# Reordering the head of a fused softcap attention and maxout MoE kernel: loads, casts and fill units ahead of the first crossbar transposes

## The chip, the cores and the metric

The kernel runs on one core of one Trainium2 chip. Times are device microseconds (us) of that core, each the median of several executions of one compiled kernel; the profile is of one execution. All executions in this study were of the fast state; within it those of one kernel still spread (the kernel before from 356.5 to 360.8 us on one chip), so a profiled execution need not be a typical one. Engines: TensorE (PE, with its weight loads PEld), VectorE (DVE), ScalarE (ACT), GpSimd (POOL), SyncE (SP, which issues nearly all DMAs; SPq marks its queue).

## The reference

```
scores = q @ k^T / sqrt(64)                 # 8 batches, 12 heads, 448 positions, 64 wide, fp32
scores = cap * tanh(scores / cap)           # cap = 30
attn   = softmax(scores)                    # exp, divided by the sum
x      = (attn @ v), heads joined           # 3584 x 768
out    = maximum(x @ w1, x @ w2) @ w_out    # 768 -> 1024 -> 768
```

The kernel computes maximum(a, b) as b + relu(a − b): it needs wd = w1 − w2 ("subtract") for the relu branch, and wm = w2 @ w_out ("premultiply"), worked out on the chip once.

## The kernel before

Two heads make a pair, three pairs a group g (16 groups), two pairs a quad t (24 quads). For groups 0 and 1 q and k are transposed by TensorE, for groups from 2 on by a DMA through the crossbar (`cross(g)`). What can be run between quads is kept as a queue of single TensorE instructions: first the transposes of w2 and the premultiply, then the MoE matmuls of each batch. `F(n)` takes n units off it. All orders are given by hand; each engine runs its instructions in the order of the program.

```python
    def load(g, what, n0=0, n1=L):       # q, k or v of pairs n0..n1 of group g, by SyncE's queue
        ...
    def cast(eng, g, what, n0=0, n1=L, halves=(0, 1)):   # fp32 -> bf16 into the buffers that matmuls read
        ...
    def load_w1(c):                      # 512 KB, by SyncE's queue
        w1_in[c] = ...
        nc.sync.dma_start(out=w1_in[c], in_=x_rows(moe_w1, c))

    def subtract(c, eng=nc.vector):
        eng.tensor_sub(wd_sb[:, c, :], w1_in[c], w2b[:, c, :])

    def cross(g):                        # q and k of a group through the crossbar
        nc.sync.dma_start_transpose(
            out=qkT_of(g).rearrange("p n j c -> p (n j) c"), in_=kqf[g % 2].rearrange("p n j c -> p (n j c)")
        )

    def add(t, ab, step):                # sums of exponentials on VectorE, for quads from NS = 3 on
        if t < NS or t >= NQ:
            return
        ...                              # six tensor_add a quad; total(t) then needs 4 matmuls in place of 16

    # ---- the order at the head ----
    load(1, "k"); load(1, "q"); load(0, "v")                # (cut: group 0's q and k, w2, w_out)
    ...
    load(1, "v")
    load(2, "k")
    load(2, "q")
    for c in range(KC):                                     # KC = 6
        load_w1(c)
    ...
    cast(nc.gpsimd, 1, "v")
    cast(nc.gpsimd, 2, "k")
    cast(nc.gpsimd, 2, "q")
    ...                                                     # (cut: quad 1's scores)
    cross(2)
    load(3, "k")
    load(3, "q")
    load(2, "v")
    ...
    for t in range(1, NQ):
        more = t + 1 < NQ
        F(24 if t == 2 else 0)
        if t > 1 and more:
            scores(t + 1, 0)                                # t == 2: quad 3, the first that needs cross(2)
        if t > 1:
            ex(t, 3)
            F(6)
        ...
        if t == 2:
            cast(nc.gpsimd, 3, "k")
            cast(nc.gpsimd, 3, "q")
            cross(3)                                        # needed by scores(4, 1), at t == 3
            for c in range(4, KC):
                subtract(c, nc.gpsimd)
        ...
        F(8 if t > 1 else 0)
        add(t, 1, 0)
        F(2 if t > 1 else 0)
        if more:
            scores(t + 1, 1)
            ex(t + 1, 0)
        ...                                                 # (cut: more adds, scores and fill)
        total(t)
        if more:
            scores(t + 1, 3)
            ex(t + 1, 2)
        else:
            F(12)
        normalize(t, values(t))                             # t == 1 is the first that needs v of group 1
        if t % 3 == 2:
            fill_q.append(moe(t // 3))
        F(3)
    F(10 ** 9)                                              # the rest of the queue
```

Of the kernel before, what the change touches and what calls it, by code (L numbers as in the profile page):

```python
# [10 lines left out]
def kernel(  # L11
# [11 lines left out]
    nc = tc.nc  # L23
# [10 lines left out]
    KC, FC = DM // P, DF // P  # L34
    NP = H // 2
    N = B * NP
    L = 3
# [64 lines left out]
    def rows(t, b, h0, h1):  # L102

        return t[b, h0:h1, :, :].rearrange("h (r j) d -> (h r) (j d)", j=R7)
# [4 lines left out]
    def raw_of(g, what):  # L109
        if (g, what) not in raw:  # L110
            if (g, what) == (1, "v"):
                raw["unused"] = raw_tile(what)
            raw[g, what] = raw_tile(what)
        t = raw[g, what]
        m = t[:, : 2 * L * NJ * D].rearrange("p (h c) -> p h c", c=NJ * D)
        l = t[:, 2 * L * NJ * D :].rearrange("p (h d) -> p h d", d=D)
        return t, m, l

    def load(g, what, n0=0, n1=L):
        b, p = divmod(g * L, NP)  # L120
        h0, h1 = 2 * (p + n0), 2 * (p + n1)
        src = {"k": k, "q": q, "v": v}[what]
        t, m, l = raw_of(g, what)
        if g < NT:
            nc.sync.dma_start(
                out=t[:, n0 * S : n1 * S].rearrange("p (n c) -> p n c", c=S),
                in_=rows(src, b, h0, h1).rearrange("(n p) c -> p n c", p=P),
            )
            return
        nc.sync.dma_start(  # L130
            out=m[:, 2 * n0 : 2 * n1, :],
            in_=src[b, h0:h1, 0 : NJ * P, :].rearrange("h (p j) d -> p h (j d)", j=NJ),
        )
        if what == "q":
            nc.sync.dma_start(
                out=l[half(b), 2 * n0 : 2 * n1, :],
                in_=src[b, h0:h1, NJ * P : S, :].rearrange("h p d -> p h d"),
            )
        else:
            for par in range(2):  # L140
                nc.sync.dma_start(
                    out=l[64 * par : 64 * par + 64, n0:n1, :],
                    in_=src[b, h0 + par : h1 : 2, NJ * P : S, :].rearrange("h p d -> p h d"),
                )

    def cast(eng, g, what, n0=0, n1=L, halves=(0, 1)):

        b = g * L // NP
        x, m, l = raw_of(g, what)
        if what == "v" and g < NT:  # L150

            x = x[:, : L * S].rearrange("p (n c) -> p n c", c=S)
            for h in halves:
                r = slice(64 * h, 64 * h + 64)
                for a in range(2):
                    eng.tensor_copy(
                        vp[g % 2][64 * a : 64 * a + 64, h::2, :, :].rearrange("p n j d -> p n (j d)"),
                        x[r, :, NJ * D * a : NJ * D * (a + 1)],
                    )
                eng.tensor_copy(vl[g % 2][r, :, r], x[r, :, 2 * NJ * D :])  # L160
            return
        if what == "v":
            eng.tensor_copy(
                vp[g % 2][:, 2 * n0 : 2 * n1, :, :].rearrange("p h j d -> p h (j d)"), m[:, 2 * n0 : 2 * n1, :]
            )
            for par in range(2):
                r = slice(64 * par, 64 * par + 64)
                eng.tensor_copy(vl[g % 2][r, n0:n1, r], l[r, n0:n1, :])
            return
        if g < NT:  # L170

            x = x[:, n0 * S : n1 * S].rearrange("p (n c) -> p n c", c=S)
            if what == "q":
                eng.tensor_copy(flat(g)[:, n0:n1, Q0 : Q0 + S], x)
                return
            eng.tensor_copy(flat(g)[:, n0:n1, : NJ * P], x[:, :, : NJ * P])
            for par in range(2):
                r = slice(64 * par, 64 * par + 64)
                eng.tensor_copy(kf[g % 2][r, n0:n1, 3, r], x[r, :, NJ * P :])
            return  # L180
        o = b % 2 if what == "q" else 0
        t = (kf if what == "k" else qf)[g % 2]
        eng.tensor_copy(  # L183
            t[:, n0:n1, o : o + NJ, :].rearrange("p n j (h d) -> p n h j d", h=2),
            m[:, 2 * n0 : 2 * n1, :].rearrange("p (n h) (j d) -> p n h j d", h=2, d=D),
        )
        if what == "q":
            eng.tensor_copy(
                t[half(b), n0:n1, 3 * (1 - o), :],
                l[half(b), 2 * n0 : 2 * n1, :].rearrange("p (n h) d -> p n (h d)", h=2),  # L190
            )
        else:
            for par in range(2):
                r = slice(64 * par, 64 * par + 64)
                eng.tensor_copy(t[r, n0:n1, 3, r], l[r, n0:n1, :])
# [24 lines left out]
    def load_w1(c):  # L220
        w1_in[c] = opool.tile([P, DF], f32, name="osb") if c < OB else w1x[:, (c - OB) * DF : (c - OB + 1) * DF]
        nc.sync.dma_start(out=w1_in[c], in_=x_rows(moe_w1, c))
# [227 lines left out]
    def F(n):  # L450
        rate[1] += n * rate[0]
        while rate[1] >= 1 and fill_q:
            try:
                next(fill_q[0])
                rate[1] -= 1
            except StopIteration:
                fill_q.pop(0)
        if not fill_q:
            rate[1] = 0.0
# [53 lines left out]
    for c in range(2, KC):  # L513
        load_w2(c)
    cast(nc.gpsimd, 0, "v", halves=(1,))
    load(1, "v")
    load(2, "k")
    load(2, "q")
    for c in range(KC):
        load_w1(c)  # L520

    first = {}
# [1 line left out]
    def premultiply_first(f0, f1):  # L524
        if f0 == 0:
            first[0] = pv_psum.tile([P, 512], f32, name="pv")
            first[1] = pv_psum.tile([P, 512], f32, name="ss")
        for f in range(f0, f1):
            for half in range(2):
                nc.tensor.matmul(  # L530
                    first[half][:, : DM // 2],
                    w2T[0][:, f * P : (f + 1) * P],
                    wo_sb[:, f, half * (DM // 2) : (half + 1) * (DM // 2)],
                    start=(f == 0), stop=(f == FC - 1),
                )
        if f1 == FC:
            for half in range(2):
                nc.vector.tensor_copy(
                    wm_sb[:, 0, half * (DM // 2) : (half + 1) * (DM // 2)], first[half][:, : DM // 2]
                )  # L540
# [7 lines left out]
    scores(1, 0)  # L548
    transposes(3)
    cast(nc.vector, 0, "v", halves=(0,))  # L550
    cast(nc.gpsimd, 1, "v")
    cast(nc.gpsimd, 2, "k")
    cast(nc.gpsimd, 2, "q")
    premultiply_first(0, 2)
    scores(1, 1)
    ex(1, 0)
# [8 lines left out]
    cross(2)  # L565
    load(3, "k")
    load(3, "q")
    load(2, "v")
    premultiply_first(6, 8)
    for c in range(1, KC):  # L570
# [10 lines left out]
    for t in range(1, NQ):  # L581
        i = 2 * t
        more = t + 1 < NQ
        F(24 if t == 2 else 0)
        if t > 1 and more:
            scores(t + 1, 0)
        if t > 1:
            ex(t, 3)
            F(6)
        if t in crosses:  # L590
            cross(crosses[t])
        if t == 2:
            cast(nc.gpsimd, 3, "k")
            cast(nc.gpsimd, 3, "q")
            cross(3)
            for c in range(4, KC):
                subtract(c, nc.gpsimd)
        if t == 3:
            cast(nc.gpsimd, 3, "v")
        if t > 2:  # L600
            extra(i)
# [6 lines that stand above are left out]
        F(4)  # L608
        add(t, 1, 1)
        F(4)  # L610
        if t == 2:
            cast(nc.gpsimd, 2, "v")
            load(3, "v")
        add(t, 0, 2)
        F(4)
        add(t, 1, 2)
        F(4)
        if more:
            scores(t + 1, 2)
            ex(t + 1, 1)  # L620
            F(5)
            add(t + 1, 0, 0)
        if t == 1:
            for c in range(4):
                subtract(c, nc.gpsimd)
        if t == 2:
            extra(4)
            extra(5)
        if t > 2:
            extra(i + 1)  # L630
        F(5)
# [4 lines that stand above are left out]
            add(t + 1, 0, 1)  # L636
        else:
            F(12)
        normalize(t, values(t))
        if casts[t]:  # L640
            nc.gpsimd.tensor_copy(mark, x_of(t, 1)[:1, :1])  # L641
            for g, what in casts[t]:
                cast(nc.gpsimd, g, what)
# [3 lines that stand above are left out]
# [34 lines left out]
```

## Time and profile before

| | before |
|---|---|
| time, median of 3 runs | 359.78 us (359.24 to 359.86) |
| span of the profiled execution | 357.5 us |
| TensorE busy, idle | 336.5, 21.0 us |
| ScalarE's last instruction ends | 306.3 us |
| from there to the end ("the tail") | 51.2 us |
| first crossbar transpose: issued, landed | 38.7, 47.9 us |
| second crossbar transpose: issued, landed | 56.1, 63.4 us |

A timeline row is: start, duration (both us, merged over the instructions at the end of the row, "x14"), engine, line, operation, result <- operands, shapes, and in brackets how long the engine sat idle before it and what released it. "us to landing" in the DMA view counts from the start of the issue to the last byte. The rows that matter are shown in the prediction; the second transpose is this row of the queue's timeline:

```profile
56.10 3.64 SPq L279 DMA_TRANSPOSE qkT<-kqf  x1
```

and the DMA view of that stretch gives it 7.3 us to landing, so 63.4.

### The profile page before, as it was taken

Reading aid. Unit: us, or ns where it says so; the run is one execution under the profiler, and the core shown is the slowest. Engines: PE = TensorE matmul, PEld = TensorE weight load, DVE = VectorE, ACT = ScalarE, POOL = GpSimd, SP = SyncE. Lnnn points to the kernel's source line nnn. Section 1 sums busy time; section 2 is a strip of 40 time slices with the busy share of each in tenths; the row PEclk is TensorE's granted clock in tenths of the full one; section 3 lists DMA queues with packets and bytes.
Section 4 is the critical chain, followed back from the end, with each engine's and each line's share of the span. In section 5 each row is a group of like instructions: output and inputs, shape, how many; then the busy total and the mean of one; then the engine's idle time right before and its main releaser. Section 6 shows DMA issues by size and latency. Waiting matters only on the chain.

```text
span 357.5 us, 6788 instructions
## 1 busy us (share of the span) xinstructions
PE 336.5 (94%) x2710; PEld 163.5 (46%) x2710; DVE 227.3 (64%) x410; ACT 281.5 (79%) x265; POOL 108.3 (30%) x172
## 2 busy tenths in 40 slices
PE   3899869899999999999999999999999999999996
PEld 2444424444444444445444554444445444455563
DVE  4336607777767776786688565976786667843421
ACT  3989639899999999999999999999999999200000
POOL 6554848231244124303430443034304400000000
PEclk9999969999999999999999999999999999999999
DMA  7999997948796869675977498948982511012022
GB/s 252 245 251 246 345 253 168 271 92 209 109 300 156 196 126 303 193 167 96 294 217 166 81 266 261 197 94 233 272 190 57 155 72 65 0 46 89 0 90 88
DMA packets 103200, 61.79 MB, mean 173 GB/s; under 512 B 62336, under 2 KB 98176, under 8 KB 103168
## 3 DMA queue, kind: packets, MB, share of 16 engines
q1 hardware_dynamic: 101216, 58.21, 62.6%
q0 software_dynamic: 1952, 3.15, 4.9%
q8 instruction: 21, 0.34, 0.4%
q14 instruction: 11, 0.09, 0.1%
HBM read 42.47 MB, written 11.01 MB: 150 GB/s over the span
## 4 chain that ended last, share of the span: by engine, by line
PE 42%; ACT 36%; DMA 13%; DVE 7%; issue 1%; SPq 0%; DVEq 0%; ACTq 0%
ACT expo L314 17%; ACT tanh L307 16%; PE mm L406 13%; PE mm L421 10%; DMA kr<-in_k_dram 9%; PE mm L418 8%; PE s L306 4%; ACT tanh L309 3%; DMA qkT<-kqf 3%; DVE gT L410 2%; PE pv L372 2%; PE ss L372 2%; DMA osb<-in_moe_w_dram 1%; DVE esum L333 1%; PE mm L243 1%
## 5 line engine op out<-in xcount | busy, mean ns | idle before, releaser
L314 ACT ACTIVATE expo<-tanh 128x1792 bf16<-128x1792 bf16 (+1 forms) x96 | 144.8, 1509 | 0.1
L307 ACT ACTIVATE tanh<-s 128x896 bf16<-128x896 f32 x144 | 124.2, 914 | 17.9 <-PE s L306 16.0
L421 PE MATMUL mm<-wo_sb,gT 128*128 128x384 bf16 x448 | 86.8, 327 | 0.0
L406 PE MATMUL mm<-xT,wd_sb 128*128 128x448 bf16 x384 | 80.2, 353 | 4.1 <-DVE gT L410 3.0
L418 PE MATMUL mm<-wm_sb,xT 128*128 128x384 bf16 x336 | 66.7, 327 | 0.2 <-DVE gT L410 0.2
L421 PEld LDWEIGHTS <-gT 128*128 128x128 bf16 x448 | 42.0, 98 | 34.2 <-issue 8.0
L406 PEld LDWEIGHTS <-wd_sb 128*128 128x128 bf16 x384 | 35.9, 98 | 44.1 <-issue 13.8
L425 DVE COPY osb<-mm 128x384 f32<-128x384 f32 x56 | 31.0, 554 | 37.0 <-PE mm L421 36.6
L306 PE MATMUL s<-qkT 64*128 64x448 bf16 x288 | 43.6, 371 | 7.7 <-DMA qkT<-kqf 4.2
L335 DVE TENSOR_TENSOR esum<-expo 128x896 bf16<-128x896 bf16 x42 | 29.4, 699 | 32.7 <-ACT expo L314 32.2
L410 DVE TENSOR_SCALAR gT<-mm 128x448 bf16<-128x448 f32 x64 | 39.6, 621 | 14.2 <-PE mm L406 13.8
L641 POOL COPY mark<-xT 1x1 bf16<-1x1 bf16 x18 | 3.2, 179 | 147.5 <-DVE xT L394 122.0
L418 PEld LDWEIGHTS <-xT 128*128 128x128 bf16 x336 | 31.8, 98 | 26.7 <-issue 6.6
L309 ACT ACTIVATE tanh<-s 128x896 bf16<-128x896 f32 x24 | 22.0, 916 | 6.0 <-PE s L301 5.5
L333 DVE TENSOR_TENSOR esum<-esum,expo 64x896 bf16<-64x896 bf16 x42 | 25.9, 617 | 0.9
L337 DVE TENSOR_TENSOR esum<-esum,expo 128x896 bf16<-128x896 bf16 x42 | 25.6, 610 | 0.3
L306 PEld LDWEIGHTS <-qkT 64*128 64x128 bf16 x288 | 9.7, 95 | 31.6 <-issue 24.2
L358 DVE STREAM_TRANSPOSE st<-ss 128x448 f32<-128x448 f32 x24 | 15.6, 649 | 8.8 <-PE ss L356 6.4
L372 PEld LDWEIGHTS <-vp 128*32 128x32 bf16 x576 | 13.3, 96 | 16.2 <-issue 8.3
L183 POOL CAST kqf<-kr 128x1152 bf16<-128x1152 f32 x14 | 15.9, 1138 | 9.0 <-DMA kr<-in_k_dram 5.0
L372 PE MATMUL pv<-expo,vp 128*32 128x448 bf16 x288 | 18.1, 356 | 0.0
L372 PE MATMUL ss<-expo,vp 128*32 128x448 bf16 x288 | 17.8, 352 | 0.0
(70 smaller groups left out, 275.5 us busy)
## 6 DMA issues: line engine op xcount, KB each, us to landing
kr<-in_k_dram SPq DMA_DIRECT2D x14, 576.0 KB, 6.6
qr<-in_q_dram SPq DMA_DIRECT2D x14, 576.0 KB, 7.1
vr<-in_v_dram SPq DMA_DIRECT2D x14, 576.0 KB, 4.9
out_dram<-osb SPq DMA_DIRECT2D x20, 384.0 KB, 4.7
out_dram<-osb SPq DMA_DIRECT2D x16, 192.0 KB, 4.2
osb<-in_moe_w_dram SPq DMA_DIRECT2D x4, 512.0 KB, 8.5
gT<-in_moe_w_dram POOLq DMA_DIRECT2D x6, 256.0 KB, 12.3
wo_sb<-in_moe_w_out_dram POOLq DMA_DIRECT2D x4, 384.0 KB, 16.2
```

What stands on the lines that cost most here:

```text
L306: nc.tensor.matmul(s[:, h, :S], k0[r, j * P : (j + 1) * P], qTn[r, :])
L307: nc.scalar.activation(tanh[t, p][:, 2 * m : 2 * m + 2, :], s[:, :, :S], AF.Tanh, scale=scale / cap)
L309: nc.scalar.activation(tanh[t, p][:, 0:2, :], s[:, :, :S], AF.Tanh, scale=scale / cap)
L314: nc.scalar.activation(expo[t, p], tanh[t, p][:, 0:n, :], AF.Exp, scale=float(cap))
L333: nc.vector.tensor_add(d, d, expo[t, 2][r, :, :])
L335: nc.vector.tensor_add(d, e_of(t, ab, 1 if ab else 0), e_of(t, ab, 2 if ab else 1))
L372: nc.tensor.matmul(ps[r, :S], vp[g % 2][:, 2 * n + h, j, u::2], e_of(t, ab, j)[:, h, :], start=(j == 0), stop=False,)
L406: nc.tensor.matmul(ps[:, :S], wd_sb[:, c, f * P : (f + 1) * P], x[:, c, cs], start=(c == 0), stop=(c == KC - 1))
L410: nc.vector.tensor_relu(g[:, f, cs], ps[:, :S])
L418: nc.tensor.matmul(ps[:, : DM // 2], x[:, c, ts], wm_sb[:, c, hs], start=(c == 0), stop=False)
L421: nc.tensor.matmul(ps[:, : DM // 2], g[:, f, ts], wo_sb[:, f, hs], start=False, stop=(f == FC - 1))
L425: nc.vector.tensor_copy(osb[:, hs], ps[:, : DM // 2])
```

## The change

The intent: the transpose that TensorE waits for should have its operands earlier (k and q of group 2 loaded ahead of two thirds of v of group 1, and cast ahead of that v), should not stand behind all of w1 (three of six chunks go behind it), and the fill kept ahead of quad 3 is cut from 24 units to 8, since the wait would be shorter. The whole diff:

```diff
     cast(nc.gpsimd, 0, "v", halves=(1,))
-    load(1, "v")
+    load(1, "v", 0, 1)
     load(2, "k")
     load(2, "q")
-    for c in range(KC):
+    load(1, "v", 1, L)
+    for c in range(3):
         load_w1(c)
...
     cast(nc.vector, 0, "v", halves=(0,))
-    cast(nc.gpsimd, 1, "v")
     cast(nc.gpsimd, 2, "k")
     cast(nc.gpsimd, 2, "q")
+    cast(nc.gpsimd, 1, "v")
...
     load(3, "k")
     load(3, "q")
+    for c in range(3, KC):
+        load_w1(c)
     load(2, "v")
...
-        F(24 if t == 2 else 0)
+        F(8 if t == 2 else 0)
...
-            for c in range(4, KC):
+            for c in range(3, KC):
                 subtract(c, nc.gpsimd)
...
         if t == 1:
-            for c in range(4):
+            for c in range(3):
                 subtract(c, nc.gpsimd)
```

Below, "the v part", "the w1 half" and "the 8 units" name its three parts.

## The prediction

> **What bounds the kernel now.** The kernel first loads and casts three heads' pairs at a time (a group), turns q and k, then runs 24 attention quads t (scores, tanh, exp, values), and lets a static queue of "fill" matmuls (the MoE part) run between them, so many units at each place. I read first the shares on the page and the waits of TensorE (us in total, times, longest):
>
> ```profile
> PE 336.5 (94%) x2710; PEld 163.5 (46%) x2710; DVE 227.3 (64%) x410; ACT 281.5 (79%) x265; POOL 108.3 (30%) x172
> ```
> ```profile
> PE s L306 <- DMA qkT<-kqf: 4.2, 1, 4.2
> ...
> PE mm L406 <- DVE gT L410: 3.0, 4, 1.3
> ```
>
> TensorE is busy nearly everywhere, so time can only come from its idle stretches and from the clock. The largest idle stretch is one wait of 4.2 us, for the first crossbar transpose (group 2's q and k, needed by quad 3). TensorE's timeline around it (start us, us, what, idle before):
>
> ```profile
> 37.45 0.55 PE L306 MATMUL s<-qkT 64*128 64x448 bf16 x4
> 37.94 0.75 PE L372 MATMUL pv<-expo,vp 128*32 128x448 bf16 x12
> ...
> 43.20 0.48 PE L243 MATMUL mm<-wo_sb,w2T 128*128 128x384 bf16 x2 [0.20 <-DVE wm_sb L248]
> 47.90 0.93 PE L306 MATMUL s<-qkT 64*128 64x448 bf16 x4 [4.21 <-DMA qkT<-kqf]
> 48.76 4.52 PE L243 MATMUL mm<-wo_sb,w2T 128*128 128x384 bf16 x14
> ...
> 53.32 0.55 PE L306 MATMUL s<-qkT 64*128 64x448 bf16 x4
> ```
>
> After the wait, 14 matmuls take 4.52 us (0.32 each, against 0.163 where 8 of them take 1.30 later): half rate, and the windows view has the granted clock at 0.50 from 48 to 52 us. So the wait costs 4.2 us and about 2.6 us of slow clock. ScalarE shows both as idle time:
>
> ```profile
> 40.81 0.95 ACT L314 ACTIVATE expo<-tanh 128x896 bf16<-128x896 bf16 x1
> 48.56 1.73 ACT L307 ACTIVATE tanh<-s 128x896 bf16<-128x896 f32 x2 [6.80 <-PE s L306]
> 50.17 1.70 ACT L314 ACTIVATE expo<-tanh 128x1792 bf16<-128x1792 bf16 x1
> 53.79 1.73 ACT L307 ACTIVATE tanh<-s 128x896 bf16<-128x896 f32 x2 [1.92 <-PE s L306]
> ```
>
> From 53.8 us to about 306 us ScalarE paces the kernel (87.3 of 90 us busy between 200 and 290), then TensorE works off the fill queue's rest to the end. Why is the transpose late? GpSimd's casts and the queue's own issues (SPq) answer:
>
> ```profile
> 25.37 1.37 POOL L156 CAST vp<-vr 64x576 bf16<-64x576 f32 x2 [2.68 <-DMA vr<-in_v_dram]
> ...
> 33.81 1.14 POOL L183 CAST kqf<-kr 128x1152 bf16<-128x1152 f32 x1 [4.97 <-DMA kr<-in_k_dram]
> 34.90 0.74 POOL L195 CAST kqf<-kr 64x192 bf16<-64x192 f32 x2
> 36.93 1.15 POOL L183 CAST kqf<-qr 128x1152 bf16<-128x1152 f32 x1 [1.28 <-DVE wm_sb L248]
> ```
> ```profile
> 38.67 7.10 SPq L279 DMA_TRANSPOSE qkT<-kqf  x1
> 45.82 0.58 SPq L130 DMA_DIRECT2D kr<-in_k_dram  x1
> ```
>
> k of group 2 lands at 33.7, q at 36.8 (issued 20.7, 16.1 us to landing), its small rest at 37.4. The transpose is issued at 38.67, but stands behind six w1 chunks of 512 KB that land from 38.8 to 44.7 by their issue times plus landing times; it lands at 47.9. The DMA share is at or over 1.0 from 10 to 44 us: here transfers bound the kernel.
>
> **What the Trainium skill says.** (1) "TensorE: Matmul & The Clock Gate", What's actually happening: TensorE falls to half clock after at least one idle window of about 3.4 us and needs about 3.4 us of activity to return. The trace agrees: 4.2 us idle, then granted clock 0.50. (2) "DMA: Bandwidth & Descriptors", Queues, rings and completion order: on each engine the descriptors of one issuing engine's ring are consumed in order. The trace agrees: the transpose lands 3.2 us after the last w1 chunk, although issued 6 us before that. (3) "SBUF — State Buffer", Who interferes with whom: a VectorE operation with two SBUF inputs contends with GpSimd's reads. The trace fits: the first esum add (L335) takes 1.63 us at 57.1, beside GpSimd's subtracts at 56.15 to 60.8, against 0.70 on average.
>
> **The change part by part.** No work is added, but for one DMA more (one load cut in two) and the same data: only order moves.
>
> *v of group 1.* 2/3 of its 672 KB (448 KB) goes behind q and k of group 2. v of group 0 lands at 20.8, of group 1 at 25.4: 4.6 us for 672 KB beside the GpSimd queue's w2 loads, so 448 KB is 3.1 us. k lands at 33.7 − 3.1 = 30.6. The w2 loads still end near 32.8, so q gains less: the displaced 448 KB then run alone at some 350 GB/s, 1.3 us, and must end where q's rest ended before, 37.4; q's rest then lands near 36.0. The casts follow at once: k at 30.6, q until about 37.1. The transpose is issued at 37.1, **1.6 us earlier**.
>
> *Half of w1 behind it.* Three chunks fewer ahead: 1.57 MB at the rate seen (3.1 MB from 37.4 to 44.7, 430 GB/s) is 3.65 us. The queue ahead of the transpose drains at 41.1 in place of 44.7; with the same 3.2 us after it, it lands at **44.3** (an estimate; it was 47.9).
>
> *v cast after q and k.* The six small casts of v (25.37 to 28.84, 3.5 us) now wait for its late part, 37.4, and end at 40.9. But the values of quad 1 need them, and TensorE comes there at 37.94. This is a **new stall of about 3.0 us**, where there was none. It is under 3.4 us, so I expect no loss of clock.
>
> *8 units in place of 24.* After the stall: values 1.6 us, then 3 + 8 units, 1.7 us: TensorE reaches quad 3's scores at 40.9 + 1.6 + 1.7 = 44.2, as the transpose lands (44.3). Then at full clock: scores 0.5, 14 matmuls and 2 transposes 2.4 us, so the next scores are there by 47.8 and ScalarE is the limit: first tanh at 44.95, 3.33 us for it and its exp, second tanh at 48.3. It was 53.79: **−5.5 us** for ScalarE's chain.
>
> *The second crossbar transpose.* k and q of group 3 are issued when the first has been issued, 42.2 (45.8 before), q's rest lands at 51.3 (54.9); three subtracts lie ahead of its casts (40.9 to 47.3), which end at 52.4. But now three w1 chunks (3.65 us) and v of group 2 (some 2 us) are in the ring ahead of it, until 57; issue ends about 1 us later, it lands 2.1 us after that, at 60.1. It landed at 63.4 before, for scores at 64.83. These scores move to 59.3. So **+0.8 us** of a new wait, for which ScalarE is the one that loses.
>
> *Quad 3 to 4.* Before, ScalarE lost 1.58 us at 70.48 after TensorE's 1.33 us wait for gT. The order of units there changes (premultiply is still running), so I count half of about 1.2: **−0.6 us**.
>
> *The tail.* The fill places give a fixed number of units as long as the queue isn't empty, and it isn't: about 80 units stand in it when ScalarE has ended. So the 16 units not run ahead of quad 3 come out at the end: 16 × 0.163 = **+2.6 us**.
>
> Sum: −5.5 + 0.8 − 0.6 + 2.6 = −2.7 us, 359.8 to **357.1 us**. Cross-check on TensorE alone: it loses the wait 4.2 and the slow clock 2.6, gains stalls of 3.0 and 0.8, net −3.0. The two agree.
>
> **The rivals.** (a) *The v stall eats it.* Were v's late part to land 1.5 us later or GpSimd's casts to be slowed, TensorE idles 4.5 us, the clock falls again, and quad 3 starts at 46 with half rate: gain of ScalarE 2 us or less, with the tail a result of 359.5 to 360. For: the transfer time is tight and GpSimd is in order. Against: total bytes ahead are unchanged. (b) *The second transpose becomes the bound.* If it lands at 62 to 63, as before, because the w1 half and v only changed places with it, then ScalarE waits 2 to 3 us: 358.5 to 360. For: 63.4 before had only 1.4 us of slack. (c) *All hidden.* v lands early enough (its 448 KB at the full 430 GB/s, casts overlapping), no stall at 70: ScalarE gains up to 6.8 + 1.9 + 1.6 = 10.3 minus a smaller wait of 2, less 2.6 tail: 354 and below. Against: bytes and GpSimd's order. (d) The subtracts, now three on GpSimd from 52.4 to 59, come late for the first L406 units or slow VectorE's adds; but 25 premultiply units now stand ahead of L406, so I give it up to 1 us.
>
> **Range and chances.** −2.7 us is 0.75%. The mistakes of the steps (transpose 1 us, stall 1 us, second wait 1.5 us, tail 0.5 us) add up to some 2.5 us: 354.2 to 359.6. Faster by over 2% needs 352.6, that is rival (c) at its fullest: 0.05. Slower by over 2% would need 7.2 us of new stalls: 0.02. Within 2%: 0.93.
>
> **What would show it.** The first transpose issued near 37 and landing near 44; a TensorE wait of about 3 us at 38 to 41 for GpSimd's v casts; the granted clock at 1.0 from 44 to 56; ScalarE's idle before quad 3 near 3 us, not 6.8, and the 1.92 us gone; a wait of up to 1 us for the second transpose near 60; ScalarE's last exp 4 to 6 us earlier and the stretch from there to the end 2.6 us longer. The prediction is wrong if the v stall passes 3.4 us, if the second transpose is over 2 us late, or if the tail doesn't lengthen because TensorE had slack in the ScalarE-paced part that takes up the 16 units.

## The result, and the profile after

| | before | after |
|---|---|---|
| time, median (6 runs each) | 359.81 us | 359.30 us |
| ratio | | 0.9993 (95%: 0.9976 to 1.0011) |
| TensorE busy, idle | 336.5, 21.0 us | 334.0, 23.5 us |
| first transpose landed | 47.9 | 45.0 |
| first tanh of quad 3 | 48.56 | 45.98 |
| second tanh of quad 3 | 53.79 | 49.32 |
| second transpose landed | 63.4 | 61.5 |
| tanh of quad 4's second scores | 65.60 | 62.95 |
| ScalarE's end | 306.3 | 302.8 |
| tail | 51.2 | 54.7 |

Nothing was gained. A ratio is the mean time of one kernel's fast runs over that of the other's in the same rounds, so not quite the ratio of the two medians. Later rounds on two other chips gave the changed kernel 1.0026 and 1.0006.

TensorE's timeline after, around the head:

```profile
37.01 0.37 PE L372 MATMUL pv<-expo,vp 128*32 128x448 bf16 x2
38.74 0.36 PE L372 MATMUL pv<-expo,vp 128*32 128x448 bf16 x1 [1.36 <-POOL vp L156]
40.55 1.30 PE L372 MATMUL pv<-expo,vp 128*32 128x448 bf16 x9 [1.45 <-POOL vp L156]
...
43.73 1.85 PE L243 MATMUL mm<-wo_sb,w2T 128*128 128x384 bf16 x10
45.51 0.55 PE L306 MATMUL s<-qkT 64*128 64x448 bf16 x4
...
56.33 0.75 PE L372 MATMUL ss<-expo,vp 128*32 128x448 bf16 x12 [1.46 <-DVE st L358]
...
61.25 1.30 PE L243 MATMUL mm<-wo_sb,w2T 128*128 128x384 bf16 x7 [1.33 <-DVE wm_sb L248]
62.48 0.55 PE L306 MATMUL s<-qkT 64*128 64x448 bf16 x4
```

TensorE's busy time counts matmuls at half clock in full: 14 of them took 4.52 us before (at 48.76 us) and 2.45 us after (at 48.69 us). That is why the idle time could rise although the wait of 4.21 us for the transpose has gone. In its place stand the stall for v (1.36 + 1.45 = 2.8 us) and, later, waits of 1.46 and 1.33 us for VectorE. The stall also cost clock, as the windows view shows (the last three columns: granted clock, DMA share, GB/s):

```profile
36.00:40.00 4.00, 1.74 (x23) 0.50 (x11) 1.54 (x3) 3.97 (x5) 3.69 (x7) 1.00 1.15 290
40.00:44.00 4.00, 3.45 (x32) 1.35 (x33) 0.87 (x2) 0.83 (x1) 3.91 (x4) 0.57 0.92 188
```

GpSimd's timeline explains the stall and half of the later waits:

```profile
31.38 1.14 POOL L183 CAST kqf<-kr 128x1152 bf16<-128x1152 f32 x1 [8.12 <-DMA kr<-in_k_dram]
...
35.54 1.15 POOL L183 CAST kqf<-qr 128x1152 bf16<-128x1152 f32 x1 [1.86 <-DMA qr<-in_q_dram]
36.75 0.51 POOL L188 CAST kqf<-qr 64x384 bf16<-64x384 f32 x1
37.32 1.37 POOL L156 CAST vp<-vr 64x576 bf16<-64x576 f32 x2
...
39.12 1.37 POOL L156 CAST vp<-vr 64x576 bf16<-64x576 f32 x2
...
52.50 2.14 POOL L225 TENSOR_TENSOR wd_sb<-osb,gT 128x1024 bf16<-128x1024 f32 x1
54.60 4.59 POOL L225 TENSOR_TENSOR wd_sb<-xT,gT 128x1024 bf16<-128x1024 f32 x2
```

The casts of k, q and v stand within 0.8 us of where the prediction put them. VectorE's additions for quad 3 (the esum rows) then fall beside the subtracts:

```profile
52.66 2.46 DVE L335 TENSOR_TENSOR esum<-expo 128x896 bf16<-128x896 bf16 x1 [0.92 <-ACT expo L314]
...
57.16 2.51 DVE L337 TENSOR_TENSOR esum<-esum,expo 128x896 bf16<-128x896 bf16 x1
```

The second addition ends at 59.67, half a microsecond after the last subtract (54.60 + 4.59 = 59.19); alone such an addition takes 0.63 us. The Trainium skill states this contention ("SBUF — State Buffer", Who interferes with whom): a VectorE operation with two SBUF inputs contends with a GpSimd operation that reads SBUF. The trace agrees: both additions ended 0.48 us after the end of a subtract, and so they did, within 0.01 us, in two more executions of the changed kernel. Below, an addition held up in this way is called locked. What TensorE needs of VectorE, the operations behind these two rows, is late by up to that much (waits of 1.46 and 1.33 us).

The second transpose has moved less than the first. Its rows in the queue's timeline and in the DMA view:

```profile
52.42 5.37 SPq L279 DMA_TRANSPOSE qkT<-kqf  x1
```
```profile
qkT<-kqf SPq DMA_TRANSPOSE x1, 9.1
```

It was issued 3.7 us earlier than before, but took 9.1 us to landing in place of 7.3, so it landed at 61.5.

On ScalarE the head is earlier, and then loses a part of it again:

```profile
45.98 1.73 ACT L307 ACTIVATE tanh<-s 128x896 bf16<-128x896 f32 x2 [5.14 <-PE s L306]
...
58.26 1.73 ACT L307 ACTIVATE tanh<-s 128x896 bf16<-128x896 f32 x2 [0.50 <-PE s L306]
...
62.95 1.73 ACT L307 ACTIVATE tanh<-s 128x896 bf16<-128x896 f32 x2 [1.38 <-PE s L306]
...
67.15 0.92 ACT L309 ACTIVATE tanh<-s 128x896 bf16<-128x896 f32 x1 [0.89 <-PE s L301]
```

The gain is 4.5 us at quad 3's second tanh, 2.65 us at quad 4's, and 3.4 us at ScalarE's end. The last rows of ScalarE, before and then after:

```profile
303.73 2.54 ACT L314 ACTIVATE expo<-tanh 128x896 bf16<-128x896 bf16 x2
```
```profile
300.29 2.54 ACT L314 ACTIVATE expo<-tanh 128x896 bf16<-128x896 bf16 x2
```

The two spans are equal (357.5 us), so the whole of these 3.4 us came back in the tail. One line of TensorE differs there, the MoE's first matmuls (from ScalarE's end to the end of the span, before and then after):

```profile
L406 PE MATMUL mm<-xT,wd_sb 128*128 128x448 bf16 x74 | 14.3, 352 | 0.0
```
```profile
L406 PE MATMUL mm<-xT,wd_sb 128*128 128x448 bf16 x82 | 16.3, 352 | 1.1 <-DVE gT L410 1.1
```

That is 8 matmuls more, and waits of 1.1 us for VectorE.

### The profile page after: what moved, and what is told of

Read it like the earlier page. It is cut to its first block, busy times and chain, and to the rows that moved or that the text cites. A ratio compares the mean times of both kernels' runs of the same rounds, so it can differ in the third digit from the quotient of the medians.

```text
span 357.5 us, 6790 instructions
## 1 busy us (share of the span) xinstructions
PE 334.0 (93%) x2710; PEld 162.9 (46%) x2710; DVE 229.0 (64%) x410; ACT 281.6 (79%) x265; POOL 109.4 (31%) x172
## 4 chain that ended last, share of the span: by engine, by line
PE 51%; ACT 29%; DVE 6%; DMA 6%; SPq 3%; issue 2%; POOL 1%; POOLq 0%; ACTq 0%; DVEq 0%
PE mm L406 16%; ACT expo L314 14%; ACT tanh L307 13%; PE mm L421 12%; PE mm L418 9%; DMA qr<-in_q_dram 5%; PE s L306 4%; SPq L141 3%; PE pv L372 3%; ACT tanh L309 2%; PE ss L372 2%; DMA kr<-in_k_dram 2%; DVE gT L410 1%; PE s L301 1%; PE mm L243 1%
## 5 line engine op out<-in xcount | busy, mean ns | idle before, releaser
L337 DVE TENSOR_TENSOR esum<-esum,expo 128x896 bf16<-128x896 bf16 x42 | 27.9, 664 | 0.3
L372 PE MATMUL pv<-expo,vp 128*32 128x448 bf16 x288 | 19.3, 363 | 2.8 <-POOL vp L156 2.8
L372 PE MATMUL ss<-expo,vp 128*32 128x448 bf16 x288 | 18.7, 362 | 1.5 <-DVE st L358 1.5
```

What stands on the lines that cost most here:

```text
L337: nc.vector.tensor_add(d, d, e_of(t, ab, 0 if ab else 2))
L372: nc.tensor.matmul(ps[r, :S], vp[g % 2][:, 2 * n + h, j, u::2], e_of(t, ab, j)[:, h, :], start=(j == 0), stop=False,)
```

## The experiments

**Theory A:** the end is TensorE's work plus its idle. The fill queue never runs empty, so units withheld at one place come out in the tail; only idle that is filled or removed counts. How much idle the 16 units withheld ahead of quad 3 would have filled is what the runs have to show. **Rival B:** ScalarE's chain sets the end and the tail has slack. **Rival C:** the earlier transpose is worth nothing, whatever is done with v and the units. Theories F and H, made later, are on what holds quad 4; other rivals are named in the expectations. Each job ran its kernels on one chip, beside runs of the kernel before: the four parts taken singly on one; the stall filled or removed, its control, and the additions alone on a second; v of group 2 alone, with the additions, with the 16 units, and the 12 units more on a third; the 16 units inside the changed kernel, and the last two runs, on a fourth. Ratios from two chips are compared with care: the changed kernel itself gave 0.9993, 1.0006 and 1.0026.

### The parts taken singly

*The changed kernel with 24 units again.*

```diff
-        F(8 if t == 2 else 0)
+        F(24 if t == 2 else 0)
```

> The changed kernel with 24 units again ahead of quad 3. Theory A (units are only traded between the head and the tail, because the fill queue never empties): quad 3's scores start 2.6 us later (48.1 in place of 45.5 us), ScalarE ends 2.6 us later, the tail is 2.6 to 3.4 us shorter, and the time is within 0.8 us of the changed kernel (358.5 to 359.8). Rival B (ScalarE's chain sets the end and the tail has slack): 2.6 us slower, 361.9.

Measured: 357.48 us, ratio 0.9965 (0.9938 to 0.9992), below the changed kernel's 0.9993, though the two intervals overlap and the changed kernel did not run on this chip. The expected 358.5 to 359.8 us was missed, and ScalarE did not end 2.6 us later but at 302.5 us (302.8 in the changed kernel). Against the lower times of this chip (359.02 before) the run is 0.35% or 1.26 us below the kernel before, at the edge of what was allowed, so it was run again beside the changed kernel on one chip, below.

*The kernel before with 8 units only.*

```diff
-        F(24 if t == 2 else 0)
+        F(8 if t == 2 else 0)
```

> The kernel before with only the 24 units made 8. Theory A: the wait for the first crossbar transpose grows from 4.2 to about 6.8 us, quad 3 starts when it did (47.9), and the 16 units come out in the tail: 2.6 us slower, 362.4. Rival B (the tail has slack): unchanged, 359.8.

Measured: 360.87 us, ratio 1.0065 (1.0044 to 1.0086), +2.3 us. The wait for the first transpose grew to 6.9 us and the tail to 54.2 us, and the time rose although ScalarE ended 1.3 us earlier (305.0 us). Theory A holds, rival B falls.

*The kernel before with the w1 half only.*

```diff
-    for c in range(KC):
+    for c in range(3):
         load_w1(c)
...
     load(3, "q")
+    for c in range(3, KC):
+        load_w1(c)
     load(2, "v")
```

(with the subtracts shared three and three, as in the change)

> The kernel before with only the w1 half put behind the first transpose (v and the 24 units as before). Theory A: the transpose lands near 44.5 to 45.5 in place of 47.9, TensorE waits about 1 to 1.5 us for it in place of 4.2, the clock stays at 1.0, no stall for v: gain 2.7 to 3.2 of the wait and 2.6 of the clock, less up to 2.5 of new VectorE waits behind GpSimd's later subtracts: 355.5 to 357.5. Rival C (the gain of an earlier transpose is lost anyway in the VectorE waits after it, whatever v does): 359 or more.

Measured: 356.85 us, ratio 0.9940 (0.9912 to 0.9968). This one part alone is worth 2.2 us, so rival C falls. But TensorE now waits twice, for both transposes:

```profile
45.36 0.80 PE L306 MATMUL s<-qkT 64*128 64x448 bf16 x4 [1.86 <-DMA qkT<-kqf]
...
64.12 0.36 PE L306 MATMUL s<-qkT 64*128 64x448 bf16 x2 [1.77 <-DMA qkT<-kqf]
```

The first landed 2.6 us earlier than before (45.3), the second, now behind half of w1, no earlier (issued at 53.55, 2.5 us sooner, but 10.5 us to landing in place of 7.3: 64.05). The clock fell after the first of these waits too, to 0.50 from 46 to 48 us, though it was of 1.86 us only.

*The kernel before with the v part only.*

```diff
-    load(1, "v")
+    load(1, "v", 0, 1)
     load(2, "k")
     load(2, "q")
+    load(1, "v", 1, L)
...
-    cast(nc.gpsimd, 1, "v")
     cast(nc.gpsimd, 2, "k")
     cast(nc.gpsimd, 2, "q")
+    cast(nc.gpsimd, 1, "v")
```

> The kernel before with only the v part (two thirds of v of group 1 loaded and all of it cast behind q and k of group 2). Theory A: a stall for v of about 2.8 us near 37 to 41 with the clock falling to near half after it, the transpose near 46.3 to 46.8, TensorE there at about 48: no gain, 358.5 to 360.5. Rival C: the earlier transpose alone is worth its 1.4 us, 358.3 or less.

Measured: 358.50 us, ratio 1.0000 (0.9972 to 1.0029). Stall for v 2.8 us, clock 0.51 from 40 to 42 us, the transpose landed at 48.7, later than expected and than before, with all of w1 still ahead of it in the queue. The v part is worth nothing.

So the parts are: w1 half −0.6%, v part 0, 8 units +0.65%. Their sum is +0.05%, the change measured −0.07% (each is known to 0.2 to 0.3% only).

### Do the 16 units cost time inside the changed kernel?

The changed kernel and the one with 24 units, on one chip:

> The changed kernel as control: ratio to before 0.999 to 1.003.

Measured: 359.14 us, ratio 1.0006 (0.9991 to 1.0021).

> The changed kernel with 24 units ahead of quad 3, on the same chip as the control. Theory A' (in the changed kernel TensorE still waits up to 1.7 us for the first transpose after the 8 units, and waits for VectorE near quad 4, so that the 16 units withheld are only partly free time lost): 0.6 to 1.7 us faster than the control, ratio 0.994 to 0.999. Rival K (a pure trade of head against tail, as first expected): within 0.2% of the control.

Measured: 356.60 us, ratio 0.9942 (0.9918 to 0.9965), 0.64% or 2.3 us faster than the control. Theory A' was expected at 0.6 to 1.7 us and gave more; rival K, the pure trade that had been expected of theory A at first, falls. ScalarE's last rows, with 8 units and then with 24:

```profile
300.82 2.54 ACT L314 ACTIVATE expo<-tanh 128x896 bf16<-128x896 bf16 x2
```
```profile
300.55 2.54 ACT L314 ACTIVATE expo<-tanh 128x896 bf16<-128x896 bf16 x2
```

ScalarE ends at 303.4 and 303.1: the 8 units gave it nothing, although quad 3's scores started at 45.59 us with them and at 47.13 without. (The two heads are not alike: in the second execution TensorE came to quad 1 4.2 us later, so that its stall for v was 0.44 us in place of 3.5 and the clock stayed at 1.00. Nothing in the edit reaches that far back.) The tails are 358.0 − 303.4 = 54.6 us and 354.8 − 303.1 = 51.7 us. So withholding 16 units makes the tail 2.9 us longer. Over all runs but the one with 12 units more, the tail is 51.2 to 51.7 us where 24 units stand ahead of quad 3 (or 8 there and 16 in the stall), and 54.2 to 54.8 us where there are 8.

### Filling the stall, and removing it

*The changed kernel with 16 units in the v stall.*

```diff
+        F(16 if t == 1 else 0)
         normalize(t, values(t))
```

> The changed kernel with 16 fill units put ahead of quad 1's values, where TensorE waits 2.8 us for the casts of v. Theory A (what the 8 in place of 24 units takes back in the tail is what is lost, the units fit into the stall): the stall shrinks to under 0.7 us, quad 3's scores wait up to 1.2 us for the transpose and start no later than in the changed kernel, the tail is 3 us shorter: 0.7 to 0.95% faster than the changed kernel, ratio to before 0.990 to 0.993. Rival D (the units delay quad 1's values and all behind them, so that it is a trade like the other): ratio 0.997 to 1.000.

Measured: 355.65 us, ratio 0.9915 (0.9890 to 0.9939). The control on this chip, the changed kernel as it is:

> The changed kernel again, as the control on this chip. Both theories: within 0.4% of the kernel before, as in the first result (ratio 0.9993).

Measured: 359.41 us, ratio 1.0026 (1.0010 to 1.0042). TensorE's timeline with the units in the stall:

```profile
37.10 1.46 PE L243 MATMUL mm<-wo_sb,w2T 128*128 128x384 bf16 x8
38.91 1.30 PE L243 MATMUL mm<-wo_sb,w2T 128*128 128x384 bf16 x7 [0.34 <-DVE w2T L235]
...
40.83 0.74 PE L372 MATMUL pv<-expo,vp 128*32 128x448 bf16 x9 [0.33 <-POOL vp L156]
...
45.47 0.55 PE L306 MATMUL s<-qkT 64*128 64x448 bf16 x4 [1.28 <-DMA qkT<-kqf]
```

The bulk of quad 1's values starts where it did (40.83 against 40.55), quad 3 starts where it did (45.47 against 45.51), so up to there the units are free. The time is 1.1% below the control's. Theory A holds, rival D falls. The profiled execution was the slowest of its eight, though (358.33 us): in it TensorE waited 2.25 us for the second transpose, the clock was at 0.50 from 64 to 66 us after that, and ScalarE ended at 304.8 us, 2.1 us after the control's. Only the tail, 51.7 us against 54.7, shows the gain there.

*The first third of v cast by itself ahead of k and q, with 24 units.* The stall is removed at its cause: quad 1 needs only this third.

```diff
+    cast(nc.gpsimd, 1, "v", 0, 1)
     cast(nc.gpsimd, 2, "k")
     cast(nc.gpsimd, 2, "q")
-    cast(nc.gpsimd, 1, "v")
+    cast(nc.gpsimd, 1, "v", 1, L)
```

(the cast of v takes the range of pairs; 24 units as above)

> The changed kernel with the first third of v of group 1, which lands early, cast by itself ahead of k and q of group 2 (quad 1 needs only that), and 24 units again. Theory A: no stall for v; TensorE reaches quad 3 at about 43 to 43.7 and waits 1.3 to 2 us for the transpose (near 45): ratio to before 0.991 to 0.9945, a little better than the w1 half alone (0.994). Rival E (the six more small casts on GpSimd delay the casts of k and q, and the transpose with them, by over 1 us): ratio 0.996 or more.

Measured: 356.43 us, ratio 0.9938 (0.9908 to 0.9968). No stall, a wait of 2.16 us for the first transpose, and the clock at 0.51 from 48 to 50 us after it. It is as good as the w1 half alone (0.9940, on another chip), no better: the v part, repaired, was not seen to bring anything. Rival E falls: the transpose was issued at 37.64 us, 37.28 to 37.57 in the changed kernel.

### What holds quad 4

*Quad 3's additions taken off VectorE.*

```diff
-    NS = 3
+    NS = 4
```

> The changed kernel with quad 3's sums of exponentials taken by TensorE from the exponentials themselves, as for quads 0 to 2, in place of six VectorE additions (12 matmuls more, 0.56 us). Theory F (VectorE's additions of quad 3, locked out by GpSimd's subtracts at 52.5 to 59, cost the waits of 1.46, 1.33 and 0.58 us and so ScalarE's 0.50, 1.38 and 0.89): these waits go, net 1.5 to 2.5 us faster than the changed kernel, ratio to before 0.992 to 0.995. Rival G (these waits only stand in for other slack): no gain or 0.5 us slower, ratio 0.999 to 1.001.

Measured: 359.95 us, ratio 1.0033 (1.0012 to 1.0054), no gain over the control's 1.0026, as rival G had it. Theory F falls as it was stated: the waits for VectorE went (the largest left is 0.2 us), but a wait for the second transpose came in their place:

```profile
60.99 0.36 PE L306 MATMUL s<-qkT 64*128 64x448 bf16 x2
63.98 0.36 PE L306 MATMUL s<-qkT 64*128 64x448 bf16 x2 [2.63 <-DMA qkT<-kqf]
```

This gave theory H, and not rival G: VectorE's locked additions and the second transpose both hold quad 4, one behind the other.

*v of group 2 loaded behind the second transpose.*

```diff
     for c in range(3, KC):
         load_w1(c)
-    load(2, "v")
...
             cross(3)
+            load(2, "v")
```

> The changed kernel with v of group 2 loaded behind the second crossbar transpose (it is not needed before quad 3's values). Theory H (two things hold quad 4 in the changed kernel near 62: VectorE's additions locked behind GpSimd's subtracts, and the second transpose, landing at 61.5; taking away one alone gives little): the transpose lands 1 to 2 us earlier, near 60, but quad 4's second scores still start at 61.8 to 62.5: ratio to before 0.998 to 1.002. Rival I (the second transpose alone is the bound): 1.5 us faster than the changed kernel, 0.995 to 0.997.

Measured: 358.92 us, ratio 0.9990 (0.9974 to 1.0007). The time lies where theory H put it. Rival I's 1.5 us is not quite excluded: the changed kernel did not run on this chip, and against its ratios of 1.0006 and 1.0026 elsewhere the gain would be 0.6 or 1.3 us. The profile can't be used for theory H: the profiled execution took 357.12 us, one of the fastest of 22 (356.5 to 360.8), and in it the additions were hardly locked (0.63 and 1.04 us). The first of them ran at 52.64 us, before the first subtract began (53.71); in the three profiled executions of the changed kernel the subtracts began at 52.5 to 52.7 and all six additions took 2.25 to 2.61 us. So the edit may have loosened this hold too; how often is open.

*Both.*

> The same with quad 3's additions taken off VectorE as well. Theory H: both holds are gone; the transpose, which landed at 63.9 with the additions removed alone and made TensorE wait 2.6 us, lands near 61.5 to 62, and the wait falls under 1 us: 0.4 to 0.8% faster than the run that removed the additions alone (1.0033), ratio 0.995 to 0.999. Rival G (those waits stand in for other slack): 1.002 or more.

Measured: 357.12 us, ratio 0.9938 (0.9915 to 0.9961), better than expected. TensorE's wait for the second transpose is 0.3 us, for VectorE 0.2. Beside the run before it on this chip, taking the additions away as well is worth 0.5%; on the other chip, taking them away alone was worth nothing. Removing either alone gave 0.999 and 1.003, removing both 0.994: theory H, and rival G falls. The four cells were not run on one chip.

### Towards a better version

*16 units in the stall, and v of group 2 behind the second transpose.*

> The run with 16 units in the v stall (ratio 0.9915), where TensorE waited 2.25 us for the second transpose at 61 to 63.4, with v of group 2 loaded behind that transpose. Theory H: it lands near 61 to 61.5, the wait falls to 0.7 us or less: ratio 0.986 to 0.9895. Rival J (the time is set elsewhere): 0.991 or more.

Measured: 355.14 us, ratio 0.9888 (0.9857 to 0.9920). TensorE's wait for the second transpose, 2.25 us with the units alone, is gone. The gain over the units alone (0.9915, on another chip) is not beyond the intervals, and rival J's 0.991 lies within this one.

*16 units in the stall, and 12 more ahead of quad 4's second scores.*

```diff
+        F(12 if t == 3 else 0)
         if more:
             scores(t + 1, 1)
```

> The run with 16 units in the v stall, with 12 more units put ahead of quad 4's second scores, into TensorE's wait of 2.25 us for the second transpose; the transpose and ScalarE's chain are left as they were. Theory A (the end is TensorE's work plus its idle, whichever engine paces the middle): the idle goes, 2 us faster: ratio 0.985 to 0.988. Rival B (ScalarE's chain sets the end): ratio 0.991 or more.

Measured: 354.90 us, ratio 0.9878 (0.9849 to 0.9908). ScalarE was not helped (it ends at 303.7 us, g1's at 301.1, where g1 is the run before), but the tail fell to 49.7 us. Two ways to work against the same wait of TensorE give the same time on one chip, though one leaves ScalarE 2.7 us later: that is what theory A says, and rival B does not.

*16 units in the stall, v of group 2 behind, additions off VectorE.*

> The changed kernel with 16 units in the v stall, v of group 2 behind the second transpose (these two 0.9888) and quad 3's additions taken off VectorE. If VectorE's locked additions still cost time in some executions: ratio 0.984 to 0.987. If not: the 12 matmuls more cost 0.5 us, ratio 0.989 to 0.991.

Measured: 354.08 us, ratio 0.9873 (0.9844 to 0.9902): between the two cases, and not to be told from the version without the third edit (0.9888, on another chip).

*The kernel before with the w1 half, and v of group 2 behind the second transpose.*

> The kernel before with the w1 half behind the first transpose (alone 0.994) and v of group 2 behind the second; v of group 1 and the 24 units as before. Theory H' (the w1 half moves its delay from the first transpose to the second, which made TensorE wait for 1.7 us of the 3.6): the second transpose lands near 62 in place of 64, ratio 0.989 to 0.9915. Rival: 0.993 or more, the second transpose's wait is replaced by another.

Measured: 353.90 us, ratio 0.9854 (0.9831 to 0.9878), better than the expected 0.989 to 0.9915, the lowest of the study (its interval overlaps those of the three before it) and the smallest edit: v of group 1 and the 24 units are left as they were. Its waits near quads 3 and 4:

```profile
45.30 0.55 PE L306 MATMUL s<-qkT 64*128 64x448 bf16 x4 [0.68 <-DMA qkT<-kqf]
...
60.84 0.55 PE L406 MATMUL mm<-xT,wd_sb 128*128 128x448 bf16 x2 [1.21 <-POOL wd_sb L225]
61.33 0.55 PE L306 MATMUL s<-qkT 64*128 64x448 bf16 x4
```

The second transpose landed at 61.3 (54.03 + 7.3), when TensorE came for it. The time is 5.2 us below that of the changed kernel on the same chip. How much of it is the second edit's is not shown: the w1 half alone (0.9940) ran on another chip, 0.9% or 3.1 us is more than the wait of 1.77 us that the edit removes, and in this profiled execution TensorE also came to quad 1 1.1 us later (38.39 against 37.27), so that it waited 0.68 us for the first transpose in place of 1.86 and kept its clock.

## Why the prediction was wrong

The time lay inside the stated range, but a gain of 2.7 us was forecast and none came. By its own steps (ScalarE's chain, profiled executions):

| step | predicted | measured |
|---|---|---|
| second tanh of quad 3 | −5.5 us | −4.5 us (53.79 to 49.32) |
| new wait up to quad 4's second scores | +0.8 us | +1.9 us (0.50 + 1.38) |
| the wait between quads 3 and 4's rest | −0.6 us | −0.7 us (1.58 to 0.89) |
| tail | +2.6 us | +3.4 us (51.2 to 54.7) |
| sum | −2.7 us | +0.1 us |

The large gain was put too high and both costs too low; only the small third term came out as it was put. So the steps that failed are the way through quad 4 ("+0.8 us" of new wait, where 1.9 us was measured) and the price of the 8 units (2.6 us of tail, where 3.4 us was measured); the head missed its 5.5 us by 1.0.

**Right.** That the first transpose was the wait, that v would become a stall near 38 to 41 us, that the transpose would be issued near 37 (37.28) and land near 44 (45.0), that the tail would lengthen, that the end is a sum on TensorE. The casts for the first transpose and its landing were worked out to within a microsecond.

**Wrong: "It is under 3.4 us, so I expect no loss of clock."** The stall was of 2.8 us, in two pieces with one matmul between them, and the clock was at 0.57 from 40 to 44 us. In another execution of the changed kernel it stayed at 1.00 there with a stall of 2.5 us; that one waited 1.65 us for the transpose instead, and quad 3 started at 45.89, no earlier than with the slow clock (45.51). So the loss of clock was real, and cost half a microsecond: TensorE came to quad 3 at 45.51, when the transpose had landed at 45.0. That landing, 45.0 to 45.9 in place of 44.3, would have held quad 3 anyway. Together they are the 1.0 us by which the first step was missed (first tanh of quad 3 at 45.98, not 44.95), about a third of the missing gain. (ScalarE's idle before quad 3, put near 3 us, was 5.14, because ScalarE also came there 0.9 us sooner than before.)

**Wrong: the second wait, "+0.8 us".** It was mis-sized and had another cause. The prediction had the second transpose land at 60.1, 7.7 us after its issue; with the w1 half and v ahead of it, it took 8.7 to 11.0 us, and landed at 61.5 in the profiled execution of the changed kernel (61.3 and 61.9 in two others, 63.9 with the additions off VectorE). And VectorE's additions, locked behind three subtracts in place of two, held TensorE longer still: in all three profiled executions of the changed kernel it came to quad 4's second scores at 62.5 to 62.7, 0.8 to 1.3 us after the transpose had landed. The prediction had both as rivals: (b) the second transpose, which it gave 358.5 to 360, and (d) the subtracts, to which it gave up to 1 us. The runs fit that one stands behind the other, so that taking away each alone moved nothing.

**Wrong: the tail.** It was priced as the 16 withheld units at 0.163 us each, 2.6 us. It grew by 3.4 us, and of other things. By the traces' records every run with 8 units has only 8 matmuls more in its tail than every run with 24, or with 8 and 16 in the stall (82 of line 406 in place of 74, as many of the others): 1.9 us of TensorE. The other 8 were worked off before ScalarE ended, since the total is the same (2710). To them come waits of 1.1 us for VectorE's gT, which no run with 24 units has there. Together they are the 2.9 us measured on one chip, within 0.1 us. The remaining 0.4 us lies behind TensorE's last matmul: from there to the end of the span it is 3.35 to 3.39 us in the four traces without the v part and 3.78 to 3.88 us in the fourteen with it. Why is open.

**The judgement behind it.** The prediction took 8 units as a trade, 2.6 us of tail against an earlier start of ScalarE, which it read as the engine that paces the kernel, being busy for 87.3 of 90 us between 200 and 290. The same view has TensorE busy for 88.87 of these 90 us. With 24 units ScalarE ended just as early (303.1 against 303.4): what it gained at quad 3 was taken back at quad 4. The withheld units therefore bought nothing and cost 2.3 us, all that the w1 half gained. VectorE's hold at quad 4 ended last in the three profiled executions of the changed kernel; whether it does in a typical one, three can't say.

## What to carry to other kernels

Where one engine works off a static queue to the end, count that engine's idle, not the chain that seems to pace the middle: fill belongs into every known wait, and units withheld come back at the end (16 of them made the tail 2.9 us longer). A load moved from ahead of one transfer to behind it goes ahead of the next one in the same queue, so follow it to the next wait; here half of w1 moved the delay from the first transpose to the second, and with v of group 2 moved behind that as well the ratio was 0.985 in place of 0.994, on two chips. When two waits stand one behind the other, remove both before you judge either.

## What the Trainium skill lacked or had wrong

- "TensorE: Matmul & The Clock Gate", What's actually happening, has the clock fall after at least one idle window of about 3.4 us. Here it fell to 0.50 after a single wait of 1.86 us (the w1 half alone) and to 0.51 after one of 2.16 us, and to 0.57 after 1.36 + 1.45 us with one matmul between; waits of 1.28 and 0.68 us left it at 1.00, and so did, in other executions, 1.00 + 1.46, 1.65, 1.77 and 2.63 us. So an idle time of a full window was not needed, and the length of one wait did not decide. The page's free-running window may be why executions differ; no run here tests it.
- "DMA: Bandwidth & Descriptors", DMA Transpose (X-bar), gives no time from issue to landing. A transpose of 128 x 24 x 128 bf16 took 5.6 us in the middle of the kernel before (the median of the 12 from 70 us on), 7.3 us for the second one there, with later loads beside it, and 8.7 to 11.0 us with three w1 chunks and v ahead of it in the queue.
- "SBUF — State Buffer", Who interferes with whom, does not say what a locked addition has still to do when it is let go: here it ended 0.48 us after the subtract, where it takes 0.63 us alone.
